# The end stage of an attention and spectral-mix kernel: a new order of tiles, 20 of 36 sums on GpSimd, six buffers, and a later place for one batch's late copies

## The chip, the cores and the metric

The kernel runs on one NeuronCore of a Trainium2 chip. The metric is the device time of one execution in microseconds (us); a comparison uses the median of several executions. A profile is taken of one further execution: it gives the start and length of every instruction on TensorE (PE; its weight loads are PEld), VectorE (DVE), ScalarE (ACT), GpSimd (POOL) and the SyncE queue (SP), which here issues every transfer, and the packets of the 16 DMA engines.

## What is computed

Eight batches, eight heads, 576 positions, 64 channels a head. First attention with a window of 128 and a linear bias; its output, with the heads side by side, is x (8 x 576 x 512). Then a spectral mix over the sequence, with 64 complex modes, and a last step with a relu:

```python
X = np.fft.rfft(x, axis=1)
Yr = np.einsum('bmd,mde->bme', Xr, w_r) - np.einsum('bmd,mde->bme', Xi, w_i)
Yi = np.einsum('bmd,mde->bme', Xr, w_i) + np.einsum('bmd,mde->bme', Xi, w_r)
...
y = np.fft.irfft(Y, n=S, axis=1)
u = x + y
return (u + np.maximum(u @ w_ch, 0.0)).astype(np.float32)
```

The output is float32, 9.44 MB. The weights w_r and w_i are 64 x 512 x 512 each in float32.

## The kernel before, in words

The program is written with a manual schedule: the instructions of each engine run in the order in which the Python code emits them, and an engine waits in that order. So the order of the code is the order of the queues, and an instruction that waits holds up all behind it on its engine.

Attention and the mix of the first channel block come first; then the weights of the other three blocks stream through a ring of three slots (L620) while TensorE multiplies each pair of modes (L694) and, between, prepares x @ w_ch for every output tile (`_xt`, `_xw`, L719 to L746). What is left for the end is `_finish`, from L815.

The end works on 36 output tiles of 128 rows by 512 channels, listed in `g.seq`. A batch has 576 rows: four whole tiles (x in `g.x_sb`) and 64 rows over. The 64 rows that are over of two batches make one shared tile (x in `g.x4`). Before the change the shared tile stands behind the second batch of its pair, so the order is batch 0, batch 1, shared 0 and 1, batch 2 and so on, and the last of the 36 is shared. A whole tile goes out in one store of 256 KB (L833), a shared one in two of 128 KB (L835).

For each tile two PSUM banks are filled by matmuls of 64 weight columns, two at a time side by side (`_halves`, L728): `mm` = u @ w_ch, from the part known before (`hl`) and ZW, and `y`, from Z. ZW and Z are, for each batch, the spectrum and the spectrum times w_ch; FT is the inverse transform. PSUM has three banks for `mm` and three for `y` (pool `fps`). `_known` begins a tile, and takes a bank that must be free; the bank of y that was released first in the program's order is taken.

A tile is finished in one of two ways, by `g.way`:

- way "a": TensorE also adds x into the y bank (so four pairs of matmuls). ScalarE writes r = relu(mm) (L855), VectorE adds o = y + r (L864).
- way "q": three pairs of matmuls, none for x. ScalarE copies y to SBUF (`ys`, L858), VectorE writes r = max(mm, x) (L859; the preparation has put x into this mm), GpSimd adds o = r + ys (L867).

Before, the way is "q" for three tiles of five, without the first two and the last five: 18 of 36. r and ys have four SBUF buffers each, o has twelve. The steps run staggered: in turn i the matmuls of tile i are emitted, then the ScalarE and VectorE step of tile i - 1, then the sum of tile i - 2; the store of an "a" tile follows its sum, that of a "q" tile one turn later.

The last modes come late, so each batch's ZW and Z are finished in the end stage: `_z_late` computes four batches at once (L779, L785; batches 0 to 3 at the start, 4 to 7 in turn 12), and `_z_take` copies one batch's 32 rows out of PSUM: ZW by ScalarE (L795), Z by VectorE (L799), or by ScalarE for batches 2 and 6 (L797). `first[b]` is the first tile that is of batch b alone; `_z_take` of batch b stands three turns ahead of it.

Of the kernel before, what the change touches and what calls it, by code (L numbers as in the profile page):

```python
# [16 lines left out]
P = 128  # L17
# [16 lines left out]
def kernel(  # L34
# [16 lines left out]
    g = Ctx()  # L51
# [37 lines left out]
    g.spectra = []  # L89
    g.seq = []  # L90
    for b in range(B):
        g.seq += [(g.x_sb[:, b, st], ((b, st * P), (b, st * P + 64))) for st in range(4)]
        if b % 2:
            g.seq.append((g.x4[:, b // 2], ((b - 1, 4 * P), (b, 4 * P))))
    g.way = ["q" if 2 <= i < len(g.seq) - 5 and i % 5 in (0, 2, 3) else "a" for i in range(len(g.seq))]

    with tc.manual_schedule(engines={ET.SP, ET.PE, ET.Activation, ET.DVE, ET.Pool}):
        with ExitStack() as wctx:
# [113 lines left out]
            for m in (NM - 4, NM - 2):  # L212
                for w in range(2):
                    _pair(g, m, w, BUSY)
                    _send(g)
            mctx.close()
        _finish(g)


# [505 lines left out]
def _halves(nc, out, lhsT, rhs, **kw):  # L725

    for h in range(2):
        nc.tensor.matmul(  # L728
            out[64 * h : 64 * h + 64], lhsT=lhsT[h], rhs=rhs[h], tile_position=(0, 64 * h), **kw)
# [41 lines left out]
def _z_late(g, b0, psum):  # L771

    nc = g.nc
    zwp = psum.tile([P, g.DM], FP32, tag="zwp", name="zwl")
    zp = psum.tile([P, 4, P], FP32, tag="zp", name="zl")
    for et in range(4):
        for c in range(4):
            l = g.ZT[:, et, 3, :, b0 + c]
            nc.tensor.matmul(  # L779
                zwp[32 * c : 32 * c + 32], lhsT=l, rhs=g.wch[:, et],  # L780
                start=(et == 0), stop=(et == 3), tile_position=(0, 32 * c))
    for et in range(4):
        for c in range(4):
            l = g.ZT[:, et, 3, :, b0 + c]
            nc.tensor.matmul(  # L785
                zp[32 * c : 32 * c + 32, et], lhsT=l, rhs=g.ident_b, start=True, stop=True,
                tile_position=(0, 32 * c))
    g.late = (zp.rearrange("p a b -> p (a b)"), zwp)


def _z_take(g, b):
    nc = g.nc
    zp, zwp = g.late
    ks = slice(32 * (b % 4), 32 * (b % 4) + 32)
    nc.scalar.copy(g.ZW[ks, b], zwp[ks])  # L795
    if b % 4 == 2:
        nc.scalar.copy(g.Z[ks, b], zp[ks])  # L797
    else:
        nc.vector.tensor_copy(g.Z[ks, b], zp[ks])  # L799


def _known(g, i):

    nc = g.nc
    x = g.seq[i][0]
    g.mm[i] = g.fps.tile([P, g.DM], FP32, tag="mm", name="mm")
    g.y[i] = g.fps.tile([P, g.DM], FP32, tag="y", name="y")
    _halves(nc, g.mm[i], [g.ident2] * 2, [g.hl[:, i, h] for h in range(2)], start=True, stop=False)
    if g.way[i] == "a":
        _halves(nc, g.y[i], [g.ident_b[:, 0:64], g.ident_b[:, 64:128]], [x] * 2,  # L810
              start=True, stop=False)


def _finish(g):

    nc, tc = g.nc, g.tc
    N = len(g.seq)
    with ExitStack() as fctx:  # L820
        pool = fctx.enter_context(tc.tile_pool(name="fin", bufs=4))
        lps = fctx.enter_context(
            tc.tile_pool(name="lps", bufs=1, space=bass.MemoryType.PSUM, side="right"))
        first = [min(i for i, t in enumerate(g.seq) if t[1][0][0] == b and t[1][1][0] == b)
                 for b in range(g.B)]
        _z_late(g, 0, lps)
        _z_take(g, 0)
        o, r, y = {}, {}, {}

        def store(i):  # L830
            for h, (b, s) in enumerate(g.seq[i][1]):
                if h == 0 and g.seq[i][1][1] == (b, s + 64):
                    nc.sync.dma_start(out=g.out[b, s : s + P, :], in_=o[i])  # L833
                    break
                nc.sync.dma_start(out=g.out[b, s : s + 64, :], in_=o[i][64 * h : 64 * h + 64])  # L835

        for i in range(N + 3):
            if i < N:
                if i >= 3:
                    _known(g, i)  # L840
                ft = [g.FT[:, b % 4, s : s + 64] for b, s in g.seq[i][1]]
                _halves(nc, g.mm[i], ft, [g.ZW[:, b] for b, _ in g.seq[i][1]],
                      start=False, stop=True)
                _halves(nc, g.y[i], ft, [g.Z[:, b] for b, _ in g.seq[i][1]],
                      start=(g.way[i] == "q"), stop=True)
            if i == first[3] - 1:
                _z_late(g, 4, lps)
            for b in range(1, g.B):
                if i == first[b] - 3:
                    _z_take(g, b)  # L850
            j = i - 1
            if 0 <= j < N:
                r[j] = pool.tile([P, g.DM], FP32, tag="r", name="r")
                if g.way[j] == "a":
                    nc.scalar.activation(r[j], g.mm[j], AF.Relu)  # L855
                else:
                    y[j] = pool.tile([P, g.DM], FP32, tag="y", name="ys")
                    nc.scalar.copy(y[j], g.y[j])  # L858
                    nc.vector.tensor_tensor(out=r[j], in0=g.mm[j], in1=g.seq[j][0], op=ALU.max)  # L859
            j = i - 2  # L860
            if 0 <= j < N:
                o[j] = pool.tile([P, g.DM], FP32, tag="o", bufs=12, name="o")
                if g.way[j] == "a":
                    nc.vector.tensor_tensor(out=o[j], in0=g.y[j], in1=r[j], op=ALU.add)  # L864
                    store(j)
                else:
                    nc.gpsimd.tensor_tensor(out=o[j], in0=r[j], in1=y[j], op=ALU.add)  # L867
            j = i - 3
            if 0 <= j < N and g.way[j] == "q":
                store(j)  # L870
# [30 lines left out]
```

## Time and profile before

| what | value |
|---|---|
| three runs, median (lowest to highest) | 443.56 us (443.05 to 444.04) |
| the profiled execution: its time, and its span | 443.07 us, 441.3 us |
| HBM traffic | 163.58 MB read, 9.44 MB written |
| share of the span busy: PE, DVE, ACT, POOL | 71%, 50%, 48%, 23% |
| chain that ended last: DMA, PE, ACT, DVE | 53%, 19%, 15%, 9% |
| last ZTa add (L703), with which the modes end | 403.40 us |
| GpSimd sums (L867) | 18, mean 1277 ns |
| ScalarE relu (L855), copy (L858), ZW copy (L795) | 18, 18 and 8; 600, 587 and 576 ns |
| VectorE max (L859), add (L864) | 18 and 18; 686 to 688 and 684 ns |
| stores: whole and half | 32 and 8; median 2.8 and 2.5 us from issue to landing |

A row of the profile names line, engine and operation, then what is written from what. In the chain of waits, each step is what released the next: a start, a length and an instruction. In a timeline the brackets give how long the engine was idle before, and whose end it waited for. A busy time can hold two instructions that overlap, so the distance between starts says more of an engine's rate than the length of one.

### The profile page before, as it was taken

The numbers are of one execution on the slowest core, as the hardware profiler recorded it, in microseconds if no ns is written. First come the engines' busy times: TensorE is split into PE (matmuls) and PEld (weight loads), VectorE is DVE, ScalarE is ACT, GpSimd is POOL, SyncE is SP. The second block draws the span as 40 slices with busy tenths as digits, with TensorE's granted clock in tenths as the row PEclk, the third lists the DMA queues.
The fourth block names the chain that finished last, engine by engine and source line by source line (L and its number), as shares of the span: only waits on it lengthen the run. The fifth ranks groups of instructions, "written<-read, shape, count | busy, mean of one in ns | idle before, by whom it ended". The sixth has DMA issues, their size and how long they took to land.

```text
span 441.3 us, 10917 instructions
## 1 busy us (share of the span) xinstructions
PE 314.4 (71%) x4624; PEld 207.7 (47%) x4652; DVE 220.4 (50%) x404; ACT 213.9 (48%) x332; POOL 103.3 (23%) x156
## 2 busy tenths in 40 slices
PE   2677788888979878457565656645576487778994
PEld 1455567666757655233333333333343255534552
DVE  6566767787747733342333324233232444512884
ACT  4799879999959603222323212222122232312883
POOL 8745535555524102000000000000000000000982
PEclk9989888999969856877867656568556889969998
DMA  8999979999999999999999999999999999993787
GB/s 288 392 393 394 403 288 403 406 405 407 404 406 405 404 419 416 418 429 427 429 429 429 420 418 423 427 426 428 430 427 429 429 427 420 429 420 140 288 310 263
DMA packets 46145, 173.73 MB, mean 394 GB/s; under 512 B 3984, under 2 KB 3984, under 8 KB 38032
## 3 DMA queue, kind: packets, MB, share of 16 engines
q1 hardware_dynamic: 46096, 173.03, 97.3%
q8 instruction: 36, 0.59, 0.5%
q14 instruction: 13, 0.11, 0.1%
HBM read 163.58 MB, written 9.44 MB: 392 GB/s over the span
## 4 chain that ended last, share of the span: by engine, by line
DMA 53%; PE 19%; ACT 15%; DVE 9%; issue 3%; SPq 0%; POOL 0%; ACTq 0%; POOLq 0%
DMA wring<-in_moe_w_i_dram 29%; DMA wring<-in_moe_w_r_dram 23%; ACT att L433 6%; ACT T L387 5%; PE acc L694 4%; DVE att L441 3%; PE mm L728 2%; PE sc L427 2%; DVE x_sb L476 2%; PE y L728 2%; PE tqk L377 2%; PE av L406 2%; PE acc L663 1%; PE av L458 1%; ACT mask L293 1%
## 5 line engine op out<-in xcount | busy, mean ns | idle before, releaser
L745 ACT CAST hl<-xw 64x512 bf16<-64x512 f32 x72 | 41.8, 580 | 140.1 <-PE xw L741 105.5
L694 PE MATMUL acc<-Xz,wring 128*128 128x32 bf16 x1536 | 51.5, 183 | 68.5 <-DMA wring<-in_moe_w_i_dram 36.6
L694 PEld LDWEIGHTS <-wring 128*128 128x128 bf16 x1536 | 45.5, 101 | 100.7 <-DMA wring<-in_moe_w_i_dram 54.9
L746 DVE TENSOR_TENSOR hl<-xw,hl 64x512 bf16<-64x512 f32 x72 | 49.6, 689 | 79.0 <-ACT hl L745 78.9
L867 POOL TENSOR_TENSOR o<-r,ys 128x512 f32<-128x512 f32 x18 | 22.5, 1277 | 240.2 <-DVE r L859 238.8
L433 ACT ACTIVATE att<-sc 128x1024 bf16<-128x1024 f32 x64 | 69.0, 1077 | 9.7 <-PE sc L427 9.1
L441 DVE TENSOR_TENSOR att<-att,mask 128x1024 bf16<-128x1024 bf16 x64 | 53.6, 838 | 36.8 <-ACT att L433 36.1
L387 ACT COPY T<-tqk 128x640 bf16<-128x640 bf16 x92 | 67.9, 801 | 2.1 <-PE tqk L377 2.1
L741 PE MATMUL xw<-wch,xT 128*128 128x512 bf16 x119 | 49.3, 533 | 4.7 <-issue 3.1
L377 PE MATMUL tqk<-ident_b,b 128*128 128x128 bf16 x432 | 41.1, 240 | 11.5 <-POOL b L367 6.4
L377 PEld LDWEIGHTS <-b 128*128 128x128 bf16 x432 | 29.1, 107 | 23.5 <-issue 11.4
L721 DVE COPY xT<-tp 128x512 bf16<-128x512 bf16 x36 | 15.1, 420 | 35.8 <-PE tp L719 35.6
L367 POOL CAST b<-v 128x576 bf16<-128x576 f32 x32 | 27.0, 868 | 20.0 <-issue 14.3
L427 PE MATMUL sc<-T,T 64*128 64x256 bf16 (+2 forms) x320 | 27.4, 269 | 2.8 <-ACT att L433 1.4
L367 POOL CAST b<-q 128x576 bf16<-128x576 f32 x32 | 21.9, 714 | 28.8 <-issue 28.8
L741 PEld LDWEIGHTS <-xT 128*128 128x128 bf16 x144 | 18.2, 132 | 22.0 <-issue 18.5
L458 PE MATMUL av<-vn,att 128*128 128x65 bf16 (+1 forms) x576 | 25.8, 206 | 0.4 <-DVE vn L410 0.3
L406 PE MATMUL av<-ident_b,T 128*128 128x128 bf16 x160 | 15.9, 236 | 13.8 <-DVE x_sb L476 7.7
L367 POOL CAST b<-k 128x576 bf16<-128x576 f32 x32 | 22.0, 716 | 12.7 <-POOL b L367 7.1
L458 PEld LDWEIGHTS <-att 128*128 128x128 bf16 (+1 forms) x576 | 21.7, 108 | 3.5 <-issue 0.2
L663 PE MATMUL acc<-X,wring 128*128 128x16 bf16 x488 | 18.9, 193 | 5.6 <-DMA wring<-in_moe_w_i_dram 4.1
L476 DVE TENSOR_TENSOR x_sb<-av,rec 128x512 bf16<-128x512 f32 x32 | 22.1, 692 | 1.1
(104 smaller groups left out, 416.7 us busy)
## 6 DMA issues: line engine op xcount, KB each, us to landing
wring<-in_moe_w_r_dram SPq DMA_DIRECT2D x32, 1536.0 KB, 10.1
wring<-in_moe_w_i_dram SPq DMA_DIRECT2D x31, 1536.0 KB, 10.1
wring<-in_moe_w_i_dram SPq DMA_DIRECT2D x22, 768.0 KB, 8.9
wring<-in_moe_w_r_dram SPq DMA_DIRECT2D x20, 768.0 KB, 8.1
q<-in_q_dram SPq DMA_DIRECT2D x32, 288.0 KB, 6.7
k<-in_k_dram SPq DMA_DIRECT2D x32, 288.0 KB, 6.6
v<-in_v_dram SPq DMA_DIRECT2D x32, 288.0 KB, 6.6
out_dram<-o SPq DMA_DIRECT2D x32, 256.0 KB, 2.8
```

The costliest lines, as they stand in the source:

```text
L367: g.nc.gpsimd.tensor_copy(u.b[w][:, :, e], u.raw[w][e])
L377: g.nc.tensor.transpose(u.tp[:, r - r0], u.b[w][:, r].rearrange("p u d -> p (u d)"), g.ident_b)
L387: copy(u.T[w].rearrange("c h (p r) -> c (h p) r", r=g.R)[:, :, r0:r1], u.tp[:, 0 : r1 - r0].rearrange("c r p -> c p r"))
L427: nc.tensor.matmul(sc[:, e, c0 : c0 + nq], lhsT=kT[es, h, _start(kt) : _start(kt) + P], rhs=qT[es, h, kt * P : kt * P + nq], start=True, s ...
L433: nc.scalar.activation(a, sc, AF.Exp, scale=1.0 / math.sqrt(g.D))
L441: nc.vector.tensor_tensor(out=a, in0=a, in1=m, op=ALU.mult)
L458: nc.tensor.matmul(av[o, h, t * (D + 1) : (t + 1) * (D + 1)], lhsT=u.att[min(kt // 2, 1), h][:, f, c0 : c0 + m], rhs=vn[:, g.ST * h + kt, ...
L476: nc.vector.tensor_tensor(out=xo, in0=avv[:, :, 0:4, 0:D], in1=rec[:, :, 0:4].unsqueeze(-1).broadcast_to([P, 2, 4, D]), op=ALU.mult)
L694: nc.tensor.matmul(acc[:, et, :, m - c0 : m - c0 + 2, :], lhsT=w[:, a].bitcast(BF16)[:, 1::2][:, et * P : (et + 1) * P], rhs=X[:, a, 1 - k ...
L741: nc.tensor.matmul(xw, lhsT=xT[:, dt], rhs=g.wch[:, dt], start=(dt == 0 and g.way[n] != "q"), stop=(dt == 3))
L745: nc.scalar.copy(g.hl[hi, n, h], xw[hi])
L746: nc.vector.tensor_tensor(out=g.hl[lo, n, h], in0=xw[hi], in1=g.hl[hi, n, h], op=ALU.subtract)
```

## The change

Four edits, all for the end stage. The shared tile of a pair moves to stand in front of the pair's batches, save for the first pair, where it stands between batch 0 and batch 1; the last tile is then a whole one. The way is "q" for two tiles of three, again without the first two and the last five, which makes 20. `fin`, the pool of r and ys, has six buffers instead of four. And the places of the late copies follow the new order: `first[b]` is the first tile that holds any row of b (0, 4, 9, 9, 18, 18, 27, 27); `_z_late` for batches 4 to 7 is still in turn 12; the copies of batches 2, 4, 6 are in turns 6, 15, 24, those of 3, 5, 7 one turn ahead of these; and those of batch 1 stay in turn 1 but stand behind the first relu there, not before it.

```diff
     for b in range(B):
+        if b == 1 or b % 2 == 0 and b:
+            c = b - b % 2
+            g.seq.append((g.x4[:, b // 2], ((c, 4 * P), (c + 1, 4 * P))))
         g.seq += [(g.x_sb[:, b, st], ((b, st * P), (b, st * P + 64))) for st in range(4)]
-        if b % 2:
-            g.seq.append((g.x4[:, b // 2], ((b - 1, 4 * P), (b, 4 * P))))
-    g.way = ["q" if 2 <= i < len(g.seq) - 5 and i % 5 in (0, 2, 3) else "a" for i in range(len(g.seq))]
+    g.way = ["q" if 2 <= i < len(g.seq) - 5 and i % 3 != 1 else "a" for i in range(len(g.seq))]
...
-        pool = fctx.enter_context(tc.tile_pool(name="fin", bufs=4))
+        pool = fctx.enter_context(tc.tile_pool(name="fin", bufs=6))
...
-        first = [min(i for i, t in enumerate(g.seq) if t[1][0][0] == b and t[1][1][0] == b)
+        first = [min(i for i, t in enumerate(g.seq) if b in (t[1][0][0], t[1][1][0]))
                  for b in range(g.B)]
...
-            if i == first[3] - 1:
+            if i == first[4] - 6:
                 _z_late(g, 4, lps)
-            for b in range(1, g.B):
-                if i == first[b] - 3:
+            for b in range(2, g.B):
+                if i == first[b] - 3 - b % 2:
                     _z_take(g, b)
             j = i - 1
...
+            if i == first[1] - 3:
+                _z_take(g, 1)
             j = i - 2
```

## The prediction

> **What bounds the kernel now.** I read the time slices first: until about 403 us the DMA row is full and the chain of waits is the weight stream, so that part is set by 173.73 MB and nothing in the change touches its transfers. The change lies in what follows, the end stage from 403.4 us (the last ZTa add) to 441.3 us. The table by windows shows how its engines stand.
>
> ```profile
> core 0: us, PE busy (x) PEld busy (x) DVE busy (x) ACT busy (x) POOL busy (x), PEclk, DMA share, GB/s
> 408.00:414.00 6.00, 5.85 (x56) 3.52 (x54) 5.58 (x10) 5.73 (x11) 5.54 (x5) 1.00 0.73 279
> 414.00:420.00 6.00, 6.00 (x78) 3.37 (x76) 4.72 (x9) 4.16 (x8) 5.14 (x5) 1.00 0.83 292
> 420.00:426.00 6.00, 5.78 (x54) 3.37 (x52) 5.37 (x9) 5.00 (x9) 5.04 (x5) 1.00 0.85 298
> 426.00:432.00 6.00, 5.66 (x53) 3.40 (x50) 5.44 (x9) 5.38 (x10) 5.60 (x6) 1.00 0.74 263
> ```
>
> Four engines are nearly full at once, and stores move 263 to 298 GB/s beside them. Which one ends last is read from the chain of waits, in three places:
>
> ```profile
> 410.31 0.59 ACT ys L858
> 410.94 0.41 PE y L728 x2
> ...
> 428.70 0.59 ACT ys L858
> 429.30 0.04 issue
> 429.34 0.41 PE y L728 x2
> ...
> 434.98 0.61 ACT r L855
> 435.61 0.69 DVE o L864
> ```
>
> The chain runs on TensorE, and hops to ScalarE where a y bank in PSUM (three of them) is still being copied out. ScalarE's own row shows why the copy of tile 5 is late:
>
> ```profile
> 408.60 0.60 ACT L855 ACTIVATE r<-mm 128x512 f32<-128x512 f32 x1
> 409.23 0.58 ACT L795 CAST ZW<-zwl 32x512 bf16<-32x512 f32 x1
> 409.71 0.57 ACT L797 CAST Z<-zl 32x512 bf16<-32x512 f32 x1
> 410.31 0.59 ACT L858 COPY ys<-y 128x512 f32<-128x512 f32 x1
> ```
>
> Two late-Z copies stand in its queue ahead of it. Last, the stores:
>
> ```profile
> 432.81 3.83 SPq L833 DMA_DIRECT2D out_dram<-o  x6
> 436.73 1.19 SPq L835 DMA_DIRECT2D out_dram<-o  x2
> ```
>
> And the windows of the same stretch:
>
> ```profile
> 434.00:439.00 5.00, 1.16 (x12) 0.45 (x7) 2.01 (x3) 1.19 (x2) 0.00 (x0) 0.97 1.05 391
> ```
>
> From 434 to 439 the DMA share is 1.05: the write-out is a full queue when the compute stops. The last add ends at 436.30, its two half stores are issued at 436.73 and 437.32, and by the DMA packets the last lands at 440.09, 3.79 us behind the add. In those packets a full store lands 0.65 us after the one ahead when queued, 1.64 us after its issue when the queue is empty, at most 2.9 us after it; the final pair took 1.38 us for one tile's bytes; and four times a gap of 1.0 to 1.3 us shows a hiccup of about 0.4 to 0.7.
>
> **The change part by part.** Prices: a pair of half matmuls starts every 0.2155 us (408.16, 408.37, 408.59). A way "q" tile has three pairs, an "a" tile four (its x is added by TensorE). A ScalarE instruction takes 0.54 us of a dense queue (424.32 to 429.19: nine), a GpSimd sum 1.235 (6.22 us for five, the last one 1.28), a VectorE one 0.60.
>
> *20 sums on GpSimd instead of 18.* TensorE loses two pairs: -0.43. ScalarE trades two relus for two copies, VectorE two adds for two maxes: nothing. GpSimd gains 2 x 1.235 = 2.47 us; its 20 sums are 24.7 from 408.28, 433.0 without a gap. In the loop before, _xw gets two more matmuls of 512 columns (about 0.5 us of PE each by the xw row, 533 ns), in a stage whose chain is weight DMA: nothing, and 0.5 if that cover were gone.
>
> *Shared tiles first, and the late copies with them.* Tile 9 now needs batches 2 and 3 together, so ZW and Z of batch 3 move from tile 10 to 5, just ahead of those of 2 at tile 6; batches 5, 4 at 14, 15, and 7, 6 at 23, 24. No copy is added; they are bunched in ScalarE's queue, and behind them stand copies that free y banks. I walk the two worst places through the queue order of the changed program, where tile 7's first y matmul waits for the copy of tile 5, and tile 25's for that of tile 23.
> First knot. ScalarE now runs ZW0, relu 0, ZW1, relu 1, copy 2, copy 3, ZW3, relu 4, ZW2, Z2, copy 5. Relu 0 starts when its matmuls end (405.97 plus 0.04); nine steps of 0.54 put copy 5 at 410.87 (before: 410.31), and 0.63 later the bank is free: 411.50. TensorE would reach that pair at 410.47: before it was there at 410.60, less two pairs (0.43), plus 0.30 for tile 4, which waits until copy 2 has ended (408.24 against 407.94). So 1.03 us of waiting, against 0.34 before (0.5 to 1.6 with steps of 0.48 to 0.60).
> Second knot. Between copies 21 and 23 ScalarE has ZW7, relu 22, ZW6, Z6: from the start of 21 to the end of 23 are 5 x 0.54 + 0.59 = 3.29 us. TensorE needs eleven pairs, 2.37 us, to the pair that waits: 0.96 if ScalarE is abreast, 1.2 if it lags by half an instruction. I take 1.1.
> A third wait, behind the second _z_late (1.27 us of TensorE that lets ScalarE catch up), costs 0.25.
> Waits on this chain before: 0.34 (410.94), 0.41 (422.52), 0.17 (426.41), 0.54 (429.34) = 1.46. After: 0.30 + 1.03 + 0.25 + 1.1 = 2.68. Added: 1.22.
>
> *Six buffers for r and y in SBUF.* They let ScalarE and VectorE run ahead of GpSimd. Waits of theirs on the GpSimd sum were 0.8 us in three on L859 and 0.3 in one on L855; none of the four TensorE waits above ends on one directly, though the 0.41 stands behind a relu whose engine had been held. The banks that TensorE waits for are PSUM, and stay three. Bounds: -0.4 to 0; I take -0.1, as the two added sums make the same queue fuller.
> The Trainium skill (Perfetto Trace Analysis, Optimization Strategy) says that a gap that repeats can mean too few SBUF or PSUM buffers for the next tile. Here it would make the six buffers worth all four waits, 1.46 us; the releaser in the rows is the copy of a PSUM bank, so I give it to a rival.
>
> *Batch 1's late Z behind the first relu.* Relu 0 starts 0.13 sooner (406.01 against 406.14), relu 1 about 0.4 later, all inside the first knot: its price is counted there. VectorE's Z copies keep their order.
>
> *The last tile is a whole one.* Before it was shared: two half stores, now one full one. SP's 40 issues stay 40, four tiles are still split.
>
> Sum to the last add: -0.43 + 1.22 - 0.1 = **+0.69**, at most +1.2 (with ScalarE at 0.60 an instruction in both knots, and nothing from the buffers). The add ends near 437.0 to 437.5 instead of 436.30.
> The write-out gives some of that back. Behind the last add stood 3.79 us; now an issue, held up to 0.43 as before (436.30 to 436.73), then 1.64 to 2.9: 1.7 to 3.4. The stores of tiles 28 to 35 still leave in a burst (GpSimd's last sum, the one SP waits for ahead of 32 to 35, comes at 433.0 plus 0.78 of waiting for copy 5 and some 0.9 at the other two knots, 434.7), so I take the upper part, 3.3 and a share of a hiccup, 0.15: 3.45, or -0.34. Forecast: 0.69 - 0.34 = **+0.35 us**. The profiled execution took 443.07 (span 441.28 and 1.79 around it), 0.49 under the median of the three runs; I add the difference to the median: 443.56 + 0.35 = 443.9, and as the bound of the sum above is farther off (+1.2) than that below, I take **444.0 us**.
>
> **The rivals.**
> *GpSimd sets the end (slower).* SP issues in order, and the store of tile 30 waits for GpSimd, with those of 32 to 35 behind it: five stores, 0.05 + 1.64 + 4 x 0.65 = 4.29 us. GpSimd decides where its last sum ends after 435.8. It idled 2.7 us among 18 sums (408.28 to 433.22, less 22.2); with that and the new 0.78 it ends at 408.28 + 24.7 + 3.5 = 436.5, the last landing at 440.8 plus a hiccup's share 0.3: +1.0, 444.6. For it: the windows, where GpSimd is at 84 to 93%. Against: five "a" tiles follow its last one, and most of its idle time was waiting for copies that a fuller queue hides.
> The Trainium skill (Perfetto Trace Analysis, Identifying the Most-Contended Engine) takes occupancy as a fair measure for GpSimd, ScalarE and VectorE and says to relieve the fullest first. By it the 2.47 us would be added whole, 446.0; I see it as the far end of this rival.
> *The knots come through whole (slower).* +1.2 at the last add and a full queue behind it: 437.5 + 0.05 + 0.43 + 2.9 = 440.9, one hiccup in three 0.2: +1.0, 444.6. For it: dense stretches of ScalarE where steps were 0.60 (409.71 to 410.31). Against: the cap of 2.9 seen in all 40 stores.
> *The waits go (faster).* If what holds the copies is GpSimd's hold on r and y, six buffers take away the 1.46, the two pairs 0.43: -1.9, 441.7. The knots must then cost nothing, so ScalarE must have been ahead at both. Against: the four rows of 408.60 to 410.31, dense with no GpSimd among the releasers.
> *That the buffers do nothing* is inside the forecast (0.1 us).
>
> **How the numbers follow.** Forecast 0.46, GpSimd 0.20, knots whole 0.17, waits gone 0.17. A measurement of this kernel can tell about 0.2% (0.89 us) from no change: the forecast is no change, both slower rivals are over it, so slower 0.37, same 0.46, faster 0.17. Range: the forecast's own is 443.2 to 444.9 (last add +0.3 to +1.2, 1.7 to 3.6 behind it, not all at once); to hold 8 in 10 I take half of the faster case and most of the slower: 442.5 to 445.2.
>
> **What would show it.** Right: TensorE waits of about 1 us for ScalarE's copies of tiles 5 and 23, the last add 0.5 to 1.2 us later, GpSimd's last sum at 434.3 to 435.5 with nearly no gap after 412, the last landing less than 3.5 us behind the add. Wrong: no such waits (then it is faster), a last sum after 435.8, or SP waiting for it while four finished tiles stand behind.

## The result, and the profile after

| | changed kernel | kernel before, in the same set of runs |
|---|---|---|
| median (lowest to highest) | 444.13 us (443.01 to 445.54) | 443.22 us (441.93 to 444.42) |
| ratio of the two, 95% interval | 1.0026 (1.0016 to 1.0036) | |
| span of the profiled execution | 442.7 us | 441.3 us |

The change makes the kernel slower by 0.26%, about 1.15 us; its interval lies around the 0.2% that a measurement of this kernel can tell from no change.

The two profiles are compared from the start of the last ZTa add (403.40 us before, 403.59 after), so that the weight stream ahead of it drops out. The last add ends 32.90 us behind it before and 34.29 after (+1.39); the last store lands 36.69 and 37.87 us behind it (+1.18). The engines in the windows of the profile after (the columns are those of the windows shown for the kernel before):

```profile
408.00:414.00 6.00, 4.79 (x42) 2.73 (x41) 4.67 (x9) 5.42 (x11) 4.39 (x4) 1.00 0.53 176
414.00:420.00 6.00, 6.00 (x76) 3.44 (x73) 5.43 (x10) 4.61 (x9) 5.54 (x5) 1.00 0.91 321
420.00:426.00 6.00, 6.00 (x56) 3.71 (x55) 5.23 (x9) 4.97 (x10) 5.83 (x5) 1.00 0.81 310
426.00:432.00 6.00, 4.79 (x45) 2.92 (x42) 4.33 (x8) 5.02 (x10) 5.44 (x6) 1.00 0.78 273
434.00:439.00 5.00, 2.74 (x26) 1.50 (x22) 3.26 (x5) 2.36 (x4) 1.58 (x2) 1.00 0.98 337
```

In two of the windows TensorE's busy time falls from 5.85 and 5.66 us to 4.79: there it stands still for over a microsecond each. The granted clock is 1.00 throughout, so it isn't slower, it waits. What it waits for is in the chain of waits of the profile after (start, length, what):

```profile
411.44 0.59 ACT ys L859
412.03 0.04 issue
412.08 0.41 PE y L729 x2
...
427.44 0.59 ACT ys L859
428.04 0.04 issue
428.08 0.41 PE y L729 x2
...
436.56 0.60 ACT r L856
437.19 0.69 DVE o L867
```

The chain makes the same hops as before, from TensorE to ScalarE's copy of a y bank and back, but TensorE waits longer at each of these two. TensorE's timeline of the changed kernel at the first place:

```profile
410.61 0.41 PE L729 MATMUL mm<-hl,ident 128*64 128x512 bf16 x2
412.08 0.41 PE L729 MATMUL y<-x_sb,ident_b 128*64 128x512 bf16 x2 [1.05 <-ACT ys L859]
```

The two pairs start 1.47 us apart instead of 0.2155, so the net wait is 1.25 us. ScalarE's timeline of the changed kernel over the same time:

```profile
409.14 0.58 ACT L796 CAST ZW<-zwl 32x512 bf16<-32x512 f32 x1
409.74 0.60 ACT L856 ACTIVATE r<-mm 128x512 f32<-128x512 f32 x1
410.36 0.58 ACT L796 CAST ZW<-zwl 32x512 bf16<-32x512 f32 x1
410.84 0.57 ACT L798 CAST Z<-zl 32x512 bf16<-32x512 f32 x1
411.44 1.07 ACT L859 COPY ys<-y 128x512 f32<-128x512 f32 x2
```

ScalarE is never idle here. The copy that TensorE needs, that of tile 5, is the first of the two in the last row; it stands behind three late copies (ZW, ZW, Z) and a relu. GpSimd is not in this chain; its own waits between 405 and 439 us of the changed kernel (us in total, times, longest; the 238 us is the idle time ahead of its first sum) are few:

```profile
POOL o L870 <- ACT ys L859: 239.6, 3, 238.1
POOL o L870 <- DVE r L860: 0.6, 1, 0.6
```

All 13 profiles of this study, in us from the last ZTa add. A net wait of TensorE is the distance between the starts of two pairs of matmuls less 0.2155; the second `_z_late`, 1.39 in each, is left out of the sum. "First" and "second" are the two places above, or what stands nearest to them: the first is at tile 7 throughout (tile 8 in e5); the second is at tile 25 under the new pattern (tile 26 in e5), at tile 29 in the kernel before, e3 and e4, and at tile 24 in e1, e10 and e11.

| kernel | GpSimd sums | waits at tile 4 | first | second | all waits | last add ends | last landing |
|---|---|---|---|---|---|---|---|
| before | 18 | 0 | 0.35 | 0.54 | 1.87 | 32.90 | 36.69 |
| changed | 20 | 0.54 | 1.25 | 1.41 | 3.73 | 34.29 | 37.87 |
| e1, order alone | 18 | 0 | 0.91 | 0.36 | 1.85 | 32.86 | 35.72 |
| e2, pattern alone | 20 | 0 | 0.78 | 0.94 | 3.58 | 34.13 | 36.85 |
| e3, batch 1 alone | 18 | 0.54 | 0.41 | 0.54 | 2.40 | 33.43 | 37.22 |
| e4, buffers alone | 18 | 0 | 0.34 | 0.54 | 1.84 | 32.91 | 35.76 |
| e5, 5 and 23 as "a" | 18 | 0.54 | 0.33 | 0.33 | 2.07 | 33.07 | 35.80 |
| e6, 6 and 24 as "a" | 18 | 0.54 | 1.04 | 1.19 | 3.30 | 34.30 | 38.18 |
| e7, Z of 2, 6 on VectorE | 20 | 0.54 | 0.77 | 0.93 | 3.02 | 33.56 | 37.01 |
| e8, batch 1 undone | 20 | 0 | 1.34 | 1.41 | 3.35 | 33.93 | 37.63 |
| e9, pattern and buffers | 20 | 0 | 0.78 | 0.91 | 3.49 | 34.07 | 36.78 |
| e10, order and buffers | 18 | 0 | 0.91 | 0.35 | 1.73 | 32.82 | 35.39 |
| e11, e10 and Z of 2 on VectorE | 18 | 0 | 0.43 | 0.35 | 1.72 | 32.79 | 35.36 |

### The profile page after: what moved, and what is told of

It is laid out like the page before. It is cut to its first block, busy times and chain, and to the rows that moved or that the text cites. A ratio compares the mean times of both kernels' runs of the same rounds, so it can differ in the third digit from the quotient of the medians.

```text
span 442.7 us, 10918 instructions
## 1 busy us (share of the span) xinstructions
PE 315.2 (71%) x4622; PEld 207.8 (47%) x4650; DVE 220.1 (50%) x404; ACT 214.6 (48%) x332; POOL 105.3 (24%) x158
## 4 chain that ended last, share of the span: by engine, by line
DMA 52%; PE 22%; ACT 14%; DVE 8%; issue 3%; SPq 0%; POOL 0%; ACTq 0%; POOLq 0%
DMA wring<-in_moe_w_i_dram 31%; DMA wring<-in_moe_w_r_dram 21%; ACT att L434 5%; ACT T L388 5%; PE acc L695 4%; DVE att L442 3%; PE mm L729 2%; PE y L729 2%; PE sc L428 2%; PE tqk L378 2%; PE xw L742 2%; DVE x_sb L477 2%; PE acc L664 2%; PE av L407 1%; PE av L459 1%
## 5 line engine op out<-in xcount | busy, mean ns | idle before, releaser
L870 POOL TENSOR_TENSOR o<-r,ys 128x512 f32<-128x512 f32 x20 | 24.8, 1273 | 240.2 <-ACT ys L859 239.6
L434 ACT ACTIVATE att<-sc 128x1024 bf16<-128x1024 f32 x64 | 67.9, 1060 | 9.3 <-PE sc L428 8.6
L388 ACT COPY T<-tqk 128x640 bf16<-128x640 bf16 x92 | 67.0, 785 | 2.1 <-PE tqk L378 2.1
```

Of the source, the lines that this page charges most:

```text
L388: copy(u.T[w].rearrange("c h (p r) -> c (h p) r", r=g.R)[:, :, r0:r1], u.tp[:, 0 : r1 - r0].rearrange("c r p -> c p r"))
L434: nc.scalar.activation(a, sc, AF.Exp, scale=1.0 / math.sqrt(g.D))
```

## The experiments

### One part of the change at a time: e1 to e4

The four edits were put into the kernel before, one each. e1 is the new order of tiles with the late copies that follow it, those of batch 1 where they were:

```diff
+        if b == 1 or b % 2 == 0 and b:
+            c = b - b % 2
+            g.seq.append((g.x4[:, b // 2], ((c, 4 * P), (c + 1, 4 * P))))
...
-                if i == first[b] - 3:
+                if i == first[b] - 3 - (b % 2 if b > 1 else 0):
```

> The kernel before with the new tile order and the new places of the late copies; 18 sums, four buffers, batch 1's copies where they were. Theory 1 (the prediction's: the late copies, bunched by the new order, fill ScalarE's queue): both knots are here, TensorE waits about 1 us for ScalarE's copy near tile 7 and again near tile 25, the last add about 0.8 us later than before, +0.4 to +0.8 us. Theory 2 (the three-turn pattern q q a makes the knots: two copies in a row behind the late ones, and the y bank of a q tile is wanted three tiles on): the first wait at most 0.8 us, the second gone, and with a whole tile at the end -0.3 to -0.9 us. Theory 3 (GpSimd's two more sums): no change within 0.2%.

Measured: 0.998 (0.9968 to 0.9992). The order alone is not slower but 0.2% faster. The first wait grows from 0.35 to 0.91 and the second shrinks from 0.54 to 0.36; the sum of waits, 1.85, is that of the kernel before, and the last add stays where it was. The waits themselves fit neither theory to the letter: 0.91 lies above the 0.8 that theory 2 allowed, and the second is smaller and elsewhere, not gone.

e2 is the new pattern of sums alone:

```diff
-    g.way = ["q" if 2 <= i < len(g.seq) - 5 and i % 5 in (0, 2, 3) else "a" for i in range(len(g.seq))]
+    g.way = ["q" if 2 <= i < len(g.seq) - 5 and i % 3 != 1 else "a" for i in range(len(g.seq))]
```

> The kernel before with 20 sums by two of three; old order, four buffers. Theory 1: two matmul pairs less and no bunching, -0.4 to 0 us, TensorE waits as before. Theory 2: waits for ScalarE's copies of 0.7 to 0.9 us at two places although the late copies stand apart, the last add 0.9 to 1.2 us later, +0.6 to +1.1 us. Theory 3: as much slower (+0.8 to +1.2), but with SP or VectorE waiting for GpSimd at the end, and its last sum behind 435.8 us.

Measured: 1.0016 (1.0003 to 1.0029), the last add 1.23 us later although two pairs (0.43 us) are gone. With the old order, TensorE's waits nearly double, from 1.87 to 3.58, which is almost the whole growth of the complete change.

e3 moves batch 1's copies behind the first relu, alone:

```diff
-            for b in range(1, g.B):
+            for b in range(2, g.B):
...
+            if i == first[1] - 3:
+                _z_take(g, 1)
```

> The kernel before with batch 1's late copies behind the first relu, nothing else. The prediction counted this at nothing by itself, inside the first knot: within 0.2%. The queue read the other way: relu 1 and the copy of tile 2 come one ScalarE step later (0.3 to 0.5 us), tile 4's x matmul waits 0.3 us for it, and the end is 0.3 to 0.6 us later.

Measured: 1.0013 (1.0003 to 1.0024), the last add 0.53 us later. Two waits of 0.28 and 0.26 us appear at tile 4, which the kernel before doesn't have.

e4 is six buffers for r and ys, alone:

```diff
-        pool = fctx.enter_context(tc.tile_pool(name="fin", bufs=4))
+        pool = fctx.enter_context(tc.tile_pool(name="fin", bufs=6))
```

> The kernel before with six buffers for r and y, nothing else. The prediction: -0.1 us (bounds -0.4 to 0), TensorE's four waits where they were. The faster rival (GpSimd's hold on r and y is what delays the copies): -1 us or more, with the waits at 422.5 and 429.3 us gone.

Measured: 0.9987 (0.9974 to 1.0), with the last add within 0.01 us of before. The interval ends at no change, and no wait of TensorE is taken away. The last landing of its profile comes 0.93 us earlier than before, as that of e1 does (0.97); this is write-out, to which the last two sections return.

The shifts of the last add, -0.04, +1.23, +0.53 and +0.01, add up to 1.73 us; the whole change has 1.39. So at the last add the pattern costs most, batch 1's place some, and the order, to which the prediction had put down the waits, nothing by itself.

### Which copy: e5 and e6

A theory in place of the fallen one: under the pattern q, q, a the copy of a "q" tile (5, and 23) stands straight behind the late copies in ScalarE's queue, and the "a" tile two places on (7, and 25) needs that bank already with its second pair of matmuls. The rival is GpSimd, which has two sums more. Both kernels are the changed one with two tiles made "a", and so both have 18 sums and the same number of matmuls; only the tiles differ.

```diff
-    ... and i % 3 != 1 else "a" ...
+    ... and i % 3 != 1 and i not in (5, 23) else "a" ...
```

> The changed kernel with tiles 5 and 23 finished the a way: 18 sums. These are the tiles whose copy stands in ScalarE's queue directly behind the late copies. Theory 2, made sharper (the knot is one copy: it frees the y bank that the a tile two places on takes with its second matmul pair): both knots fall below 0.4 us although TensorE has two more pairs; last add 33.2 to 33.5 us behind the last ZTa add (before 32.90, changed 34.29), time -0.5 to -1.1 us against the changed kernel, so within 0.2% of before. Theory 3 (what counts is the number of GpSimd sums): the same as with tiles 6 and 24.

Measured: 1.0 (0.999 to 1.0011). The waits of 1.25 and 1.41 at the x pairs of tiles 7 and 25 shrink to 0.07 and 0.23, and one of 0.33 each appears on an mm bank, at tiles 8 and 26. ScalarE's timeline in e5 shows why:

```profile
409.93 0.58 ACT L796 CAST ZW<-zwl 32x512 bf16<-32x512 f32 x1
410.41 0.57 ACT L798 CAST Z<-zl 32x512 bf16<-32x512 f32 x1
411.01 0.60 ACT L856 ACTIVATE r<-mm 128x512 f32<-128x512 f32 x1
411.50 0.58 ACT L859 COPY ys<-y 128x512 f32<-128x512 f32 x1
```

Behind the late copies there is a relu, and the pair of tile 7 that had waited runs without waiting, as TensorE's timeline of e5 shows:

```profile
410.40 0.41 PE L729 MATMUL mm<-hl,ident 128*64 128x512 bf16 x2
410.68 0.41 PE L729 MATMUL y<-x_sb,ident_b 128*64 128x512 bf16 x2
```

e6 excludes tiles 6 and 24 instead:

```diff
-    ... and i % 3 != 1 else "a" ...
+    ... and i % 3 != 1 and i not in (6, 24) else "a" ...
```

> The changed kernel with tiles 6 and 24 finished the a way: 18 sums as well, the same matmuls and copies in number as with 5 and 23. Theory 2: copies 5 and 23 stand where they stood, both knots stay at 0.9 to 1.3 us, last add 34.1 to 34.4, time like the changed kernel (+0.15 to +0.35% against before). Theory 3: two sums less as with 5 and 23, so faster by as much as that.

Measured: 1.0036 (1.0022 to 1.0051), as slow as the whole change. TensorE's timeline of e6:

```profile
409.85 0.41 PE L729 MATMUL mm<-hl,ident 128*64 128x512 bf16 x2
411.10 0.41 PE L729 MATMUL y<-x_sb,ident_b 128*64 128x512 bf16 x2 [0.84 <-ACT ys L859]
```

The wait is there, 1.04 us net, and the last add ends at 34.30, as in the changed kernel (34.29) with its 20 sums. Taking two sums off GpSimd gives TensorE two more pairs (0.43 us), and its waits are 0.43 us shorter, so this pair of kernels alone would not decide. But e5 has the same number of sums and of pairs as e6, and its last add ends 1.23 us earlier: what counts is where the copy stands, not how many sums GpSimd has. That settles GpSimd's rival for this change. (The ratios of e5 and e6 differ by 0.36%, about 1.6 us; besides the last add, the write-out of the two profiles differs, 2.73 against 3.88 us.)

### What stands ahead of the copy: e7 and e8

e7 is the changed kernel with the Z copies of batches 2 and 6 on VectorE, one ScalarE step less ahead of the copies of tiles 5 and 23.

```diff
-    if b % 4 == 2:
+    if b < 0:
```

> The changed kernel with Z of batches 2 and 6 copied by VectorE, not ScalarE: one step fewer ahead of copies 5 and 23. Theory 2: each knot shorter by one step, 0.5 to 0.6 us, last add 33.1 to 33.4, time -0.8 to -1.1 us against the changed kernel. If instead the PSUM banks were held by something else (VectorE's adds, GpSimd), VectorE's longer queue makes it the same or slower.

Measured: 1.0007 (0.9994 to 1.0021). Both long waits shrink by 0.48 us each, to 0.77 and 0.93. ScalarE's timeline of e7, to be set beside the one of the changed kernel:

```profile
409.44 0.58 ACT L796 CAST ZW<-zwl 32x512 bf16<-32x512 f32 x1
410.04 1.07 ACT L859 COPY ys<-y 128x512 f32<-128x512 f32 x2
```

The copy follows ZW2 directly. The wait is thus the queue ahead of one copy: take one step out, and TensorE waits for one step less. The last add comes 0.73 us earlier, at 33.56, a little less than was expected.

e8 undoes batch 1's place in the changed kernel.

```diff
-            for b in range(2, g.B):
-                if i == first[b] - 3 - b % 2:
+            for b in range(1, g.B):
+                if i == first[b] - 3 - (b % 2 if b > 1 else 0):
...
-            if i == first[1] - 3:
-                _z_take(g, 1)
```

> The changed kernel with batch 1's late copies ahead of the first relu again. From the edit by itself (+0.53 at the last add): tile 4's wait of 0.37 and the one before it gone, the knots as they were (1.2 and 1.4), last add 33.8 to 34.0, time -0.3 to -0.5 us against the changed kernel.

Measured: 1.0031 (1.0019 to 1.0043), not told apart from the whole change. In the profile the waits at tile 4 are gone (0.54), the first long wait grows a little (1.34 against 1.25), and the last add ends 0.36 us earlier. The profile shows a gain that the medians don't confirm.

### The buffers again, and versions that beat both: e9 to e11

e9 is the kernel before with the new pattern and six buffers (the diffs of e2 and e4).

> The kernel before with the new pattern of GpSimd sums and six buffers for r and y, old order of tiles. With the pattern alone the trace had three TensorE waits of 0.50 us on an mm bank (at 11.47, 19.95 and 27.83 us of the end stage) and the last add at 34.13. Theory A, that these three are relus held by GpSimd's grip on r and y, and that six buffers take them away: no mm wait of 0.50, last add 32.6 to 33.4, ratio 0.998 to 1.000. Theory B, that the buffers do nothing here either (they did not move the last add alone): the waits stay, last add 34.0 to 34.2, ratio 1.001 to 1.003. Theory C, that the freed time runs into the waits on y copies, since GpSimd and ScalarE are full: the mm waits go, the y waits grow by as much, last add 33.8 to 34.3, ratio 1.001 to 1.003.

Measured: 1.0004 (0.9991 to 1.0017), the last add at 34.07: theory B by the trace. The three mm waits are still there (0.42 net each, at 11.43, 19.92 and 27.77). The median alone, between the bounds of A and B, would not decide. e8, which is e9 with the new order and its copies, has none of these three, so the new order takes them away; in exchange both long waits grow, from 0.78 and 0.91 to 1.34 and 1.41. At the last add the order is then worth 0.14 us (34.07 to 33.93). VectorE's waits between 405 and 439 us (us in total, times, longest) show what the buffers did. Those of e2:

```profile
DVE r L859 <- PE mm L728: 2.1, 3, 0.8
DVE Z L799 <- PE zl L785: 1.7, 2, 1.5
DVE r L859 <- POOL o L867: 1.6, 3, 0.9
```

And those of e9, over the same time:

```profile
DVE r L859 <- PE mm L728: 3.7, 5, 1.2
DVE Z L799 <- PE zl L785: 1.6, 2, 1.4
```

The 1.6 us in which VectorE waited for GpSimd to free a buffer are gone, and 1.6 us of waiting for TensorE's mm have come in their place. VectorE was early either way. The last add moves by 0.06 us here, 0.01 and 0.04 under the old pattern (e4, and e10 against e1). The medians of e4 and e9 lie a little lower than those without the buffers, but their intervals overlap with them.

e10 is e1 and e4 together, and e11 adds the Z copy of batch 2 on VectorE:

```diff
-    if b % 4 == 2:
+    if b == 6:
```

> The kernel before with the new order of tiles and its copies, and six buffers; the old pattern of 18 sums and batch 1's copies where they were. The order alone measured 0.998, the buffers alone 0.9987 with an unmoved last add. If the two add: 0.9967, last add about 32.8. If the buffers are worth nothing under the old pattern: 0.998, last add 32.8 to 32.9. If buffers hurt by letting ScalarE run relus ahead of late copies: over 0.999, last add over 33.2.

> As the one with order and buffers, and Z of batch 2 copied by VectorE instead of ScalarE. The first knot of the order alone (0.99 us at 8.11, TensorE waiting for the copy of tile 5) has Z2's step of 0.48 to 0.60 ahead of it in ScalarE's queue. Theory of the knot: it shrinks to 0.4 to 0.5, last add 32.3 to 32.6, ratio 0.995 to 0.998. If the time lost at the first knot is regained later anyway (TensorE waits at the second one instead), last add 32.8 to 32.9 and the ratio is that of order and buffers. If VectorE is as full there as ScalarE: its adds and maxes come later, mm waits appear, last add over 32.9.

Measured: e10 0.9986 (0.9974 to 0.9997), so the two do not add; e11 0.9962 (0.9942 to 0.9982, from 7 runs against 12 of e10), which at 441.31 us against 443.17 is the fastest of all. By these ratios both beat the kernel before, and with it the changed one. But e11's end stage is that of e10, 35.36 and 35.39 us to the last landing: the first wait shrinks from 0.91 to 0.43 as the theory said, and waits of 0.28, 0.10 and 0.08 us appear just behind it, so that the sum stays at 1.72 against 1.73. That its median is 0.98 us lower than e10's is not explained by the end stage, and the intervals overlap; that it is the better of the two is not shown.

## Why the prediction was right or wrong

**The time was met, by luck; the size of the change was not.** The sum had +0.35 us and 0.44 was forecast; measured is 1.15, and 1.18 at the last landing of the two profiles. The forecast of 444.0 lies near 444.13 because the kernel before measured 443.22 here, 0.34 below the median that the forecast was added to. By its mechanism and size, the rival in which the knots come through whole is what happened: it had +1.2 at the last add and +1.0 in all, against +1.39 and +1.18.

**The bound and the places: right.** TensorE waits at the x pair of tiles 7 and 25 for the copies of tiles 5 and 23, as walked; TensorE lost two pairs (121 to 119); GpSimd's last sum ends at 435.58, which is 435.39 against the ZTa add of before, inside 434.3 to 435.5. Three of the signs did not come: the last add is 1.39 us later, not 0.5 to 1.2; GpSimd still paused for 0.63 and 0.56 us after 412; and the last landing stands 3.58 us behind the add, not under 3.5.

**The cause of the added time: wrong.** The step that failed is the one that said of the new order "No copy is added; they are bunched in ScalarE's queue", charged the added waits to it, and priced the pattern, besides the two pairs, at nothing. The walk through the queue used the new pattern without saying so: that tile 5 is "q" and tile 7 "a" is part of what makes it wait so long. e1 has the bunching without the pattern and its waits sum to 1.85; e2 has the pattern without the bunching and 3.58. The pattern moves the last add by 1.23 us alone (e2), by 1.16 with the buffers (e4 to e9) and by 1.11 with the order and the buffers (e10 to e8). The order moves it by -0.04 alone and by -0.14 with the pattern and the buffers (e9 to e8). So the bunching does lengthen the two knots, as the prediction walked them, but it shortens other waits by as much. This holds for the last add; the medians of e9 and e8, 1.0004 and 1.0031, go the other way with intervals that do not overlap, and so do their last landings (36.78 and 37.63).

**The size of the waits: too small.** On the predicted list the waits went from 1.46 to 3.33 and not to 2.68: 0.54 instead of 0.30 at tile 4, 1.25 instead of 1.03, 0.13 instead of 0.25 behind `_z_late`, 1.41 instead of 1.1. The term that was mis-sized is ScalarE's step. It was taken as 0.54 us from a dense stretch with fewer late copies. From relu 0 (406.33) to the copy of tile 5 (411.44) nine steps took 5.11 us, 0.568 each; from the copy of tile 21 (424.52) to that of tile 23 (427.44) five took 2.92, 0.584 each. Of these fourteen steps ten are long, 0.59 to 0.63, and all ten lead into or out of a late copy (the last section has the rows). Also relu 0 did not start 0.13 us earlier, as the sum had it, but as far behind the ZTa add as before (2.74 us).

**Batch 1's copies: wrong.** They were priced inside the first knot. Alone they cost 0.53 us at the last add, at tile 4 and not at the knot (e3); in the whole change, where part of it would be waited for at the knot anyway, 0.36 (e8).

**The buffers: right in size, nothing at the last add.** The row that decided was the releaser, a PSUM bank. The Trainium skill (Perfetto Trace Analysis, Optimization Strategy) reads a repeated gap as a possible shortage of SBUF or PSUM buffers. Here the SBUF half of that rule gave nothing in three pairs of runs (0.01, 0.04 and 0.06 us at the last add), and no run here tried a fourth y bank.

**GpSimd as the bound: rightly made a rival, and it fell.** GpSimd is busy 5.83 of 6 us in the window from 420. By the Trainium skill (Perfetto Trace Analysis, Identifying the Most-Contended Engine) that occupancy would make it the engine to relieve first. e6 relieves it by two sums, for two more pairs on TensorE, and its last add does not move; e5, relieved by as many at the same price, ends 1.23 us earlier.

**The write-out: 3.58 us behind the add against 3.45, but the reason is not borne out.** The give-back of 0.34 rested on the last tile leaving in one store. Over the 13 profiles the landing stands 2.56, 2.57, 2.73, 2.86, 3.45, 3.58, 3.70 and 3.88 us behind the last add where the last tile is a whole one, and 2.71, 2.73, 2.85, 3.79 and 3.80 where it is shared. The groups overlap fully. What order alone gains, 0.83 us between its medians, is not explained by the waits: its last add moved by 0.04 us, and the rest in its profile is write-out. The write-out is not mere scatter, though. With the twelve measured ratios turned into us (times 443.2), they lie 0.30 us in the mean from the shifts of the last landing, and 0.53 us from those of the last add. So a part of what the runs differ by (e1, e4, e9 above all) is decided behind the last add, and no experiment here was made for that part.

## What to carry to other kernels

Where two engines hand small buffers to one another, moving work between engines also changes which instruction stands behind a burst in an in-order queue; write out that queue and ask who needs the first hand-over behind the burst, and how soon. An engine at 97% of a window can still be off the path: two kernels with equal work on every engine, differing only in where it stands, tell the two apart. Undo each part of a mixed change alone before naming its cause, since a time that is met can carry a wrong cause; then undo it in the company of the others too, since its effect there can differ.

## What the runs showed of the hardware that was not expected

ScalarE's steps on rows of 512 come in two lengths. In the changed kernel the distance between starts is 0.48 to 0.49 us from a relu to a y copy (407.55 to 408.04) and from a ZW to a Z copy (410.36 to 410.84), but 0.60 to 0.62 from ZW to relu (409.14 to 409.74), relu to ZW (409.74 to 410.36) and Z to y copy (410.84 to 411.44). In all 13 profiles the length goes with the partition at which a row begins. A tile's row begins at partition 0, and the late copies of batch b at 32 times b % 4. Counted were the steps between rows without idle time, in which all that the second row waits for had come over 0.25 us before its start. Where the two begin at different partitions, the 80 steps took 0.596 to 0.654 us, and the second row started 0.02 to 0.03 us after the first had ended. Where they begin at the same one, the 75 steps took 0.465 to 0.494, and the second row started before the first had ended. The late copy of batch 4, which begins at partition 0, shows that it isn't the kind of row that decides; in the changed kernel it stands between a relu and a y copy:

```profile
418.50 0.60 ACT L856 ACTIVATE r<-mm 128x512 f32<-128x512 f32 x1 [0.49 <-PE mm L729]
419.00 0.56 ACT L796 CAST ZW<-zwl 32x512 bf16<-32x512 f32 x1
419.46 1.13 ACT L859 COPY ys<-y 128x512 f32<-128x512 f32 x2
```

No run changed the partition alone, and why it counts the runs don't show. A mean from another stretch was off by 5 to 8% here (0.568 and 0.584 against 0.54), since the knots hold more such changes.

The last landing scatters by over a microsecond behind the same last add. In the changed kernel most of the last stores land 0.65 us behind the one ahead, and the very last 1.24 us; in e1 the last seven all land 0.65 to 0.74 us behind the one ahead. It goes with one DMA packet that is no store, the last 8 KB packet of the queue that the profile lists as "q14 instruction". In the six kernels in which it lies among the last stores and takes 0.49 to 1.09 us (before, changed, e3, e6, e7, e8), the last landing stands 3.45 to 3.88 us behind the last add. In the seven in which it takes 0.31 us (e1, e2, e9) or starts after the last landing (e4, e5, e10, e11), it is 2.56 to 2.86. The two agree without exception, but no run moved that packet, so that it is the cause is not shown.
